# Two first w1 blocks between the scalings of v of steps 0 and 2, v of step 1 scaled on VectorE, v of block 1 in quarters, 40 leading zero matmuls

## The chip, the cores and the metric

One core of a Trainium2 chip runs the whole kernel. The metric is device time in microseconds: 230.68 us is the median of four runs before the change (231.03, 228.87, 230.79, 230.57). The profiled execution took 231.03 us, of which 228.8 us is the span from its first to its last recorded instruction.

## The reference

The inputs are q, k and v of 4 batches, 8 heads, 768 positions and 64 features, one decay `lam` per head, and two weight matrices. A linear attention with decay comes first, then a feed-forward layer:

```python
for b in range(nb):                      # blocks of 64 positions
    intra = einsum('bhic,bhjc->bhij', qb, kb) * Dmask          # lam ** (i - j), i >= j
    intra = einsum('bhij,bhjd->bhid', intra, vb)
    inter = einsum('bhid,bhde->bhie', qb * lam_pow, kv_state)
    out[:, :, sl] = intra + inter
    kv_state = lam_block * kv_state + einsum('bhsd,bhse->bhde', kb * rev_pow, vb)
x = out.transpose(0, 2, 1, 3).reshape(3072, 512)
h = x @ w_in                             # 512 x 2048
s = sin(alpha * h)
return (h + s * s / (alpha + 1e-9)) @ w_out                    # 2048 x 512
```

## The kernel before

**Tiling.** The kernel works on blocks of 128 positions and on pairs of batches. A block of a pair with one half of the heads is a "step"; there are 24, and steps 0 and 1 are the two head halves of block 0, steps 2 and 3 those of block 1. For a step, TensorE transposes q and k (T, line 444), multiplies them (S, line 453), and VectorE or ScalarE writes the transposes to `qkT` (line 623) and the masked product to `S_m` (line 568, or, for step 3 alone, ScalarE to `S_raw` at line 564 and VectorE at line 565). Then come the outputs of the step: `S_m` times the scaled v (line 466), the state from earlier blocks (line 476), and the new state from k and the scaled v (line 489). VectorE puts the output, with its decay, into `xT` (line 581) and adds up the state in `Zacc` (line 602); the next block reads the state as `Zs`.

**Scaling of v.** `prep_v(s)` (line 416) multiplies the v of step s, 128 x 512 float32 as it was loaded, by a table of decays `Lv` and writes it as bfloat16 to `v2`. It is one instruction (line 423) on the engine that the call names: POOL (GpSimd) or VectorE. Without it the output part of step s can't start.

**Feed-forward.** Four steps make a chunk of 512 tokens. `grp_A` multiplies `xT` of the chunk by 128 columns of w1 (four matmuls of 128x512, line 640), ScalarE takes the sine (line 644), one of three engines squares it (lines 651, 652) and VectorE forms `gT` (line 654); a chunk has 16 such groups. `grp_B` multiplies `gT` by w2 (line 677). Chunk 0 needs `xT` of steps 0 to 3, so its stage A ends the opening.

**Loads.** In the opening every large load is issued by POOL: k and q of blocks 0 and 1, v of blocks 0 and 1 (`load`, line 298), and w1 in four blocks (`w1_block`, line 405), which convert float32 to bfloat16 on the way. One issue occupies POOL's sequence about as long as a short computation. v of block 0 comes in quarters (`by_step=True`: two halves of the heads, each in two batches), v of block 1 in halves, by batch.

**Order.** No loop decides what an engine runs next. The program records operations with an estimated duration; `Program.add` gives each a planned start from its dependencies, the engine's free time and a model of the loads, and every engine's instructions are then sorted by planned start. Lines 715 to 760 record the opening by hand. An engine works through its list in order and waits on semaphores. `sec` records one or more parts of steps (t transposes, s product, o output); with `later=True` it hands back the part for VectorE and ScalarE as a function to call later. `P.ops[-1]` is the operation recorded last; a load given `after=[...]` waits for it.

`idle_pe(n)` (line 379) records n matmuls of 128x128 by 128 columns on a tile of zeros at the start; nothing reads their result.

Of the kernel before, what the change touches and what calls it, by code (L numbers as in the profile page):

```python
# [27 lines left out]
class Program:  # L28
# [57 lines left out]
    def add(self, eng, fn, dur, reads=(), writes=(), slot=None, nbytes=0, after=()):  # L86
        op = Op(eng, fn, dur, len(self.ops))
        self.ops.append(op)
        op.deps = self.deps_of(reads, writes) | set(after)
        for b in reads:  # L90
            if b.startswith("b."):
                op.deps.update(r for r in self.readers.get(b, ()) if r.eng != eng)
        for b in reads:
            self.readers.setdefault(b, []).append(op)
        for b in writes:
            self.writer[b] = op
            self.readers[b] = []
        op.nbytes = nbytes
        t = self.ready(eng, op.deps)
        if slot is None:  # L100
            op.start = self.place(eng, t, dur)
            op.end = op.start + dur
            return op
        op.slot = slot
        self.slots[slot] = self.slots.get(slot, 0) + 1
        op.kslot = self.slots[slot]
        issue = self.ISSUE[eng] * (0.85 if 10000 < nbytes < 100000 and eng == "POOL" else 1)
        op.start = self.place(eng, max(t, self.issued[eng]), issue)
        self.issued[eng] = op.start
        if nbytes < 10000:  # L110
            op.end = op.start + 2.9
        else:
            self.dma_free = max(self.dma_free, op.start + self.BEGIN) + nbytes / self.RATE
            op.end = self.dma_free + self.DONE
        return op
# [72 lines left out]
def bass_lightning_attn__then__act_snake_kernel(  # L188
# [31 lines left out]
    with es:  # L220
# [50 lines left out]
        P = Program()  # L271
        rec = P.add
        def bk(*ids):
            return [f"b.{i}" for i in ids]
# [9 lines left out]
        def fastest(choices, reads, writes, after=()):  # L284
            def end(c):
                eng, dur = c
                deps = P.deps_of(reads, writes) | set(after)
                return P.probe(eng, P.ready(eng, deps), dur) + dur
            return min(choices, key=end)

        def half(r):
            return slice(64 * r, 64 * r + 64)

        def where(s):
            pair, n, hh = s // 12, (s % 12) // 2, s % 2
            return pair, n, hh

        def load(d, x, after=(), by_step=False, eng=None, us=(0, 1)):
            pair, n = d // NB, d % NB
            r = d % RL  # L300
            src, dst = {"k": (k, k2), "q": (q, q2), "v": (v, v32)}[x]
            ops = []
            for h0, h1 in ((0, HS), (HS, H)) if by_step else ((0, H),):
                for u in us:
                    a = bass.AP(src.tensor, ((2 * pair + u) * H + h0) * S * D + n * BL * D,
                                [[2 * D, 64], [S * D, h1 - h0], [1, 2 * D]])
                    keys = [f"{x}.{r}.{u}.{h // HS}" for h in range(h0, h1, HS)]
                    op = rec(eng or ("SP" if x == "v" else "POOL"),
                             lambda e, u=u, a=a, h0=h0, h1=h1: e.dma_start(dst[r][half(u), h0:h1, :], a), 0,  # L309
                             writes=keys, slot=f"{x}{r}{h0 if by_step else ''}{'p' if eng else ''}",  # L310
                             nbytes=(187000 if d < 2 else 150000) if x != "v" else 216500 // (2 if by_step else 1), after=after)
                ops.append(op)
            return ops if by_step else op
# [6 lines left out]
        def consts():  # L320
            rec("ACT", lambda e: e.dma_start(lam_bc[:, :], bass.AP(lam.tensor, 0, [[0, 128], [1, H]])), 0,
                writes=["lam"], slot="lam", nbytes=4096)
            rec("ACT", lambda e: e.preload_act_table_set("natural_log_exp_and_others"), 1.3, writes=["table"])
            rec("ACT", lambda e: e.dma_start(alpha_r[:, :], moe_alpha.rearrange("(m p) -> m p", p=128)), 0,
                writes=["alpha_r"], slot="alpha", nbytes=8192)
            rec("DVE", lambda e: e.memset(maskf[:, :], 0.0), 0.2, writes=["maskf"])
            rec("ACT", lambda e: e.activation(lnlam[:, :], lam_bc[:, :], ACTF.Ln), 0.3,
                reads=["lam", "table"], writes=["lnlam"])
            for c in range(2):
                rec("ACT", lambda e, c=c: e.activation(lnlamp[half(c), :], lam_bc[half(c), c:H:2], ACTF.Ln), 0.3,  # L330
                    reads=["lam", "table"], writes=[f"lnlamp.{c}"])
# [13 lines left out]
        def iotas():  # L345
            rec("POOL", lambda e: e.iota(X_i[:, :, :], [[1, 2], [2, 64]], base=0, channel_multiplier=0), 0.2,
                writes=["X_i"])
            rec("POOL", lambda e: e.iota(N_i[:, :], [[BL, NB]], base=0, channel_multiplier=0), 0.1, writes=["N_i"])
            rec("POOL", lambda e: e.iota(E_i[:, :, :, :], [[BL, NB], [0, H], [1, 2]], base=0, channel_multiplier=2), 0.2,
                writes=["E_i"])  # L350

        def identf_op():
            rec("POOL", lambda e: e.affine_select(
                out=identf[:, :], in_=maskf[0:NM, 0:NM], pattern=[[-1, NM]], compare_op=ALU.not_equal, fill=1.0,
                base=0, channel_multiplier=1), 0.3, reads=["maskf"], writes=["identf"])
# [23 lines left out]
        def idle_pe(n):  # L379
            z = maskf[:, :].bitcast(BF16)  # L380

            def pe(e):
                for _ in range(n):
                    last = e.matmul(PS[:, 0, 0:128], z[:, 0:128], z[:, 128:256])
                return last
            rec("PE", pe, 0.06 * n, reads=["maskf"], writes=bk(0))
# [15 lines left out]
        def w_load(fn, keys, slot, n, after):  # L402
            return rec("POOL", fn, 0, writes=keys, slot=slot, nbytes=131072 * n, after=after)

        def w1_block(m0, n, after=()):
            cs = slice(128 * m0, 128 * (m0 + n))
            src = moe_w_in[:, cs].rearrange("(c p) f -> p c f", p=128)
            return w_load(lambda e: e.dma_start(w1[:, :, cs], src), [f"w1.{m}" for m in range(m0, m0 + n)],
                          f"w1_{m0}", n, after)
# [6 lines left out]
        def prep_v(s, engs=("POOL", "DVE")):  # L416
            pair, n, hh = where(s)
            c, r = s % RC, s // 2 % RL
            src = v32[r][:, HS * hh:HS * hh + HS, :].rearrange("p h (t d) -> p (h t) d", t=2)
            L_b = bass.AP(Lv, (n * H + HS * hh) * 2, [[NB * H * 2, 128], [1, 2 * HS], [0, D]])  # L420
            reads, writes = part_keys("v", s) + ["Lv"], [f"v2.{c}"]
            eng, dur = fastest([(e, {"POOL": 1.05, "DVE": 0.65}[e]) for e in engs], reads, writes)
            rec(eng, lambda e: e.tensor_tensor(v2[c][:, :, :], src, L_b, ALU.mult), dur, reads=reads, writes=writes)  # L423
# [7 lines left out]
        def part_keys(x, s):  # L431
            return [f"{x}.{s // 2 % RL}.{u}.{s % 2}" for u in range(2)]
# [282 lines left out]
        load(0, "k")  # L715
        load(0, "q")
        consts()
        idle_pe(16)
        iotas()
        consts3()  # L720
        load(1, "k")
# [3 lines left out]
        sec(t=1, tb=(2, 3), t_engs=("ACT",))  # L725
        consts2()
        load(0, "v", eng="POOL", by_step=True)
        load(1, "v", eng="POOL")
        identf_op()
        decay_table(0, 2)  # L730
        sec(s=0, sb_=4)
# [2 lines left out]
        sec(t=3, tb=(2, 3), t_engs=("ACT",))  # L734
        decay_table(2, NB)
        prep_v(0, ("POOL",))
        prep_v(1, ("POOL",))
        zl = []
        sec(s=2, sb_=0)
        o0 = sec(o=0, ob=4, z_late=zl, later=True)  # L740
        w1_block(0, 3, after=[P.ops[-1]])
        w1_block(3, 5)
        sec(s=3, sb_=2, via=True)
        o0()
        sec(o=1, ob=6, z_late=zl)
        prep_v(2, ("POOL",))
        prep_v(3, ("POOL",))
        w1_block(8, 4)
        w1_block(12, 4)
        o2 = sec(o=2, ob=0, later=True)  # L750
        o3 = sec(o=3, ob=2, later=True)
# [120 lines left out]
```

## Time and profile before

| quantity | us |
|---|---|
| median of four runs | 230.68 |
| profiled execution | 231.03 |
| its span | 228.8 |
| TensorE matmuls busy | 207.1 (91%) |
| VectorE busy | 144.0 (63%) |
| ScalarE busy | 125.1 (55%) |
| POOL busy, DMA issues among it | 117.7 (51%) |
| first matmul of stage A of chunk 0 starts | 23.44 |
| stage B of chunk 0 starts | 40.34 |

The page gives busy times over the whole span, then forty slices of it. TensorE is busy for nine tenths or more of nearly every slice from the fifth on; in the first four (some 5.7 us each) it is not. The timeline of an engine lists its instructions with start, duration, line and count; a bracket gives the idle time ahead of a group and what ended it. The chain of waits lists, in order of time, the work that each later piece had to wait for.

### The profile page before, as it was taken

The page shows a single profiled execution, that of the slowest core. Times are in us where ns is not written, and L with a number is a line of the kernel's source. Part 1 is how long each engine was busy: PE and PEld are TensorE (multiplying, and loading weights), DVE is VectorE, ACT ScalarE, POOL GpSimd, SP SyncE. Part 2 cuts the span into 40 slices and gives each one's busy share as a digit, 9 for nine tenths or more (in the row PEclk, how much of TensorE's full clock was granted, in tenths as well). Part 3 has the DMA queues.
Part 4 walks back from the last instruction along what each step waited for, and adds up shares of the span by engine and source line. Part 5 has one row for each costly group of instructions (what it writes and reads, how often), then busy time and mean ns, then how long its engine had stood idle before and what let it go on. Part 6 is the DMA issues. An engine that isn't in the chain of part 4 may idle for free.

```text
span 228.8 us, 6389 instructions
## 1 busy us (share of the span) xinstructions
PE 207.1 (91%) x2784; PEld 107.9 (47%) x2817; DVE 144.0 (63%) x205; ACT 125.1 (55%) x194; POOL 117.7 (51%) x154
## 2 busy tenths in 40 slices
PE   3465999989999989999999999999999999999994
PEld 2354343454544455644455544465544554444453
DVE  2764489548379957658765678766478764378400
ACT  4853389341399833477826477634577442568130
POOL 8978991233446554375664476653465500555300
PEclk9999999999999999999999999999999999999999
DMA  7959999972899985950179930198200104101033
GB/s 68 158 148 145 206 186 191 250 131 25 105 176 258 187 81 147 154 127 0 46 69 168 185 91 3 46 84 198 49 0 1 46 6 95 46 0 46 3 92 92
DMA packets 42891, 23.49 MB, mean 103 GB/s; under 512 B 26848, under 2 KB 39408, under 8 KB 42864
## 3 DMA queue, kind: packets, MB, share of 16 engines
q0 software_dynamic: 30240, 12.59, 43.6%
q1 hardware_dynamic: 12368, 10.42, 18.2%
q8 instruction: 22, 0.36, 0.7%
q10 hardware_dynamic: 256, 0.08, 0.2%
q14 instruction: 5, 0.04, 0.1%
HBM read 27.28 MB, written 6.29 MB: 147 GB/s over the span
## 4 chain that ended last, share of the span: by engine, by line
PE 78%; DVE 9%; POOL 5%; issue 3%; DMA 2%; ACT 1%; POOLq 0%; DVEq 0%
PE PS L677 32%; PE PS L640 31%; DVE gT L654 5%; PE PS L444 5%; PE PS L476 3%; PE PS L466 3%; PE PS L453 2%; DMA v<-in_v_dram 2%; DVE u L652 2%; PE PS L704 2%; POOL k L309 1%; PE PS L489 1%; POOL v L423 1%; DVE S_m L568 1%; POOL q L309 1%
## 5 line engine op out<-in xcount | busy, mean ns | idle before, releaser
L640 PE MATMUL PS<-xT,w 128*128 128x512 bf16 x376 | 88.5, 388 | 1.5 <-DVE Zacc L602 1.0
L654 DVE SCALAR_TENSOR_TENSOR gT<-u,r_sb,PS 128x512 bf16<-128x512 bf16 x96 | 69.7, 746 | 25.4 <-POOL u L652 21.7
L677 PE MATMUL PS<-w,gT 128*128 128x512 bf16 x343 | 81.9, 379 | 3.8 <-issue 3.6
L644 ACT ACTIVATE t<-PS,alpha_sb 128x512 bf16<-128x512 f32 x96 | 63.6, 682 | 22.8 <-PE PS L640 22.4
L652 POOL TENSOR_TENSOR u<-t 128x512 bf16<-128x512 bf16 x44 | 45.4, 1051 | 35.2 <-ACT t L644 32.3
L640 PEld LDWEIGHTS PS<-xT,w 128*128 128x128 bf16 x384 | 37.4, 100 | 49.3 <-issue 4.9
L677 PEld LDWEIGHTS PS<-w,gT 128*128 128x128 bf16 x368 | 33.9, 98 | 39.6
L568 DVE TENSOR_TENSOR S_m<-PS,mask 128x1024 bf16<-128x1024 f32 x23 | 28.1, 1224 | 22.1 <-PE PS L453 22.1
L623 ACT COPY qkT<-PS 128x1024 bf16<-128x1024 bf16 x21 | 21.2, 1011 | 28.8 <-PE PS L476 19.2
L684 ACT COPY osb<-PS 128x512 f32<-128x512 f32 x23 | 13.5, 585 | 29.5 <-PE PS L677 29.4
L309 POOL DMA_DIRECT2D k<-in_k_dram x24 | 16.9, 709 | 19.0 <-PE PS L677 12.5
L423 POOL TENSOR_TENSOR v<-v,Lv 128x512 bf16<-128x512 f32 x16 | 17.0, 1070 | 18.0 <-DMA v<-in_v_dram 16.9
L581 DVE TENSOR_TENSOR xT<-PS,Xt 128x512 bf16<-128x512 f32 x24 | 16.4, 685 | 11.7 <-PE PS L476 10.9
L444 PE MATMUL PS<-ident,q 64*64 64x64 bf16 x384 | 14.3, 205 | 6.7 <-POOL ident L316 5.0
L309 POOL DMA_DIRECT2D q<-in_q_dram x24 | 16.6, 701 | 5.7 <-PE PS L677 4.1
L651 ACT ACTIVATE u<-t 128x512 bf16<-128x512 bf16 x28 | 17.6, 630 | 1.4
L466 PE MATMUL PS<-S_m,v 64*64 64x128 bf16 x384 | 14.3, 235 | 3.6 <-POOL v L423 3.3
L652 DVE TENSOR_TENSOR u<-t 128x512 bf16<-128x512 bf16 x24 | 14.6, 610 | 4.4 <-ACT t L644 4.4
L444 PEld LDWEIGHTS PS<-ident,q 64*64 64x64 bf16 x384 | 9.6, 114 | 16.5 <-issue 11.9
L604 POOL CAST Zs<-Zacc 128x256 bf16<-128x256 f32 x16 | 7.5, 472 | 17.2 <-DVE Zacc L602 17.2
L476 PE MATMUL PS<-qkT,Zs 64*64 64x128 bf16 x160 | 15.5, 232 | 0.4
L453 PE MATMUL PS<-qkT 64*64 64x128 bf16 x384 | 12.6, 233 | 1.4 <-DVE qkT L623 0.8
(50 smaller groups left out, 129.5 us busy)
## 6 DMA issues: line engine op xcount, KB each, us to landing
out_dram<-osb SPq DMA_DIRECT2D x46, 128.0 KB, 2.8
v<-in_v_dram SPq DMA_DIRECT2D x16, 256.0 KB, 4.9
k<-in_k_dram POOLq DMA_DIRECT2D x24, 128.0 KB, 4.0
q<-in_q_dram POOLq DMA_DIRECT2D x24, 128.0 KB, 4.3
w<-in_moe_w_out_dram POOLq DMA_DIRECT2D x4, 512.0 KB, 12.5
v<-in_v_dram POOLq DMA_DIRECT2D x6, 256.0 KB, 12.3
w<-in_moe_w_in_dram POOLq DMA_DIRECT2D x2, 512.0 KB, 8.5
w<-in_moe_w_in_dram POOLq DMA_DIRECT2D x1, 640.0 KB, 7.4
```

The source lines that it names most:

```text
L309: lambda e, u=u, a=a, h0=h0, h1=h1: e.dma_start(dst[r][half(u), h0:h1, :], a), 0,
L423: rec(eng, lambda e: e.tensor_tensor(v2[c][:, :, :], src, L_b, ALU.mult), dur, reads=reads, writes=writes)
L444: last = e.transpose(dst, part((q2, k2)[x], t, u, h, tt), ident[half(u), half(u)])
L466: return e.matmul(dst, v2[o % RC][half(u), hid(h, tj), :], S_m[o % RS][half(u), h % 2 ^ u, h // 2, tj, :], start=start, stop=True, skip_gr ...
L476: return e.matmul(dst, Zs[(o - 2) % 3][half(r), u, h // 2, :], qkT[o % RQ][half(r), u, 0, h // 2, :], start=start, stop=True, skip_group_c ...
L568: rec("DVE", lambda e: e.tensor_tensor(s_out, s_in, mask_b, ALU.mult), 1.25, reads=keys_s + ["mask.0", "mask.1"], writes=[f"S_m.{s % RS}"])
L623: rec(eng, lambda e: (e.copy if eng == "ACT" else e.tensor_copy)(to, ti), dur, reads=keys_t, writes=[f"qkT.{j}"])
L640: last = e.matmul(PS[:, i, :], w1[:, kc, 128 * m:128 * (m + 1)], xT[x][:, kc, :], start=(kc == 0), stop=(kc == NKC - 1))
L644: rec("ACT", lambda e: e.activation(t16[tt][:, :], PS[:, i, :], ACTF.Sin, scale=alpha_sb[:, m:m + 1]), 0.7, reads=bk(i) + ["alpha"], write ...
L652: return e.tensor_tensor(u16[tt][:, :], t16[tt][:, :], t16[tt][:, :], ALU.mult)
L654: rec("DVE", lambda e: e.scalar_tensor_tensor(out=gT[g][:, m, :], in0=u16[tt][:, :], scalar=r_sb[:, m:m + 1], in1=PS[:, i, :], op0=ALU.mul ...
L677: last = e.matmul(PS[:, bank, :], gT[g][:, m, 128 * s4:128 * (s4 + 1)], w2[:, m, :], start=(m == 0), stop=(m == NM - 1))
```

## The change

Four edits in the opening and one in the model of issue times:

- `idle_pe(16)` becomes `idle_pe(40)`.
- v of block 1 is loaded in quarters, as v of block 0 is: four issues of 128 KB on POOL for two of 256 KB.
- The scaling of v for step 1 goes from POOL to VectorE; it is recorded after the product of step 2.
- w1 is loaded in blocks of 4, 4, 4 and 4 groups for 3, 5, 4 and 4. The first two are issued right after the scaling of step 0 (the first waits for it), the third waits for the scaling of step 3. Before, the first waited for the last TensorE operation of the output of step 0.
- In the model, an issue of 10,000 to 120,000 bytes on POOL counts 0.82 of the usual time; before it was 0.85, up to 100,000 bytes. Only the quarters of v, at 108,250 bytes, fall under the new bound.

`s3 = sec(..., later=True)` followed at once by `s3()` records the same operations in the same order as the one call did.

```diff
-        issue = self.ISSUE[eng] * (0.85 if 10000 < nbytes < 100000 and eng == "POOL" else 1)
+        issue = self.ISSUE[eng] * (0.82 if 10000 < nbytes < 120000 and eng == "POOL" else 1)
...
-        idle_pe(16)
+        idle_pe(40)
...
-        load(1, "v", eng="POOL")
+        load(1, "v", eng="POOL", by_step=True)
...
         prep_v(0, ("POOL",))
-        prep_v(1, ("POOL",))
+        w1_block(0, 4, after=[P.ops[-1]])
+        w1_block(4, 4)
         zl = []
         sec(s=2, sb_=0)
+        prep_v(1, ("DVE",))
         o0 = sec(o=0, ob=4, z_late=zl, later=True)
-        w1_block(0, 3, after=[P.ops[-1]])
-        w1_block(3, 5)
-        sec(s=3, sb_=2, via=True)
+        s3 = sec(s=3, sb_=2, via=True, later=True)
+        s3()
         o0()
         sec(o=1, ob=6, z_late=zl)
         prep_v(2, ("POOL",))
         prep_v(3, ("POOL",))
-        w1_block(8, 4)
+        w1_block(8, 4, after=[P.ops[-1]])
         w1_block(12, 4)
```

## The prediction, made before the changed kernel was run

> **What bounds the kernel now.** I read the forty slices of the page first:
>
> ```profile
> PE   3465999989999989999999999999999999999994
> ```
>
> From the fifth slice (22.9 us) TensorE is full almost throughout. Work that begins earlier there ends earlier; only the opening has room. So next comes the chain of waits of the opening:
>
> ```profile
> 8.72 1.77 POOL v L309 x3
> 10.49 4.79 DMA v<-in_v_dram
> 15.28 0.07 issue
> 15.35 1.04 POOL v L423
> 16.39 1.57 POOL w L408 x2
> 17.97 1.44 POOL v L423
> 19.41 0.04 issue
> ...
> 22.29 0.69 DVE xT L581
> 22.98 0.34 DVE Zacc L602
> 23.32 0.12 issue
> 23.44 6.16 PE PS L640 x15
> ```
>
> POOL carries the chain from 15.35 to 19.41 us: it scales v of step 1, issues two w1 loads, scales v of step 2. TensorE's output of step 2 waits for that. Then steps 2 and 3 run, and stage A of chunk 0 begins at 23.44. POOL's timeline shows its neighbours:
>
> ```profile
> 8.63 3.91 POOL L309 DMA_DIRECT2D v<-in_v_dram  x6
> 12.47 0.19 POOL L353 TENSOR_SCALAR_AFFINE_SELECT identf<-maskf 16x16 f32<-16x16 f32 x1
> 14.10 1.04 POOL L423 TENSOR_TENSOR v<-v,Lv 128x512 bf16<-128x512 f32 x1 [1.44 <-DMA v<-in_v_dram]
> 15.35 1.04 POOL L423 TENSOR_TENSOR v<-v,Lv 128x512 bf16<-128x512 f32 x1 [0.21 <-DMA v<-in_v_dram]
> 16.39 1.58 POOL L408 DMA_DIRECT2D w<-in_moe_w_in_dram  x2
> 17.96 2.45 POOL L423 TENSOR_TENSOR v<-v,Lv 128x512 bf16<-128x512 f32 x2
> ```
>
> The bracket 1.44 is idle time before step 0's scaling. The last line is steps 2 and 3: 1.44 us and 1.04 us by the chain and the row's median.
>
> A second loss lies inside stage A. TensorE's timeline there:
>
> ```profile
> 26.42 2.95 PE L640 MATMUL PS<-xT,w 128*128 128x512 bf16 x7
> 28.56 2.75 PE L640 MATMUL PS<-xT,w 128*128 128x512 bf16 x11
> ```
>
> Up to about 28.7 us a 128x512 matmul follows the last every 0.43 us, afterwards every 0.22 us, though the page's row of granted clock reads 9 throughout. From 23.44 to 28.7 only some 12 matmuls run, three groups of 16.
>
> [...] 5.3 us of stage A pass at half rate, then the rate doubles; the 16 zero matmuls (1.17 to 3.06 us) released nothing. [...] step 2's scaling took 1.44 instead of 1.04 us, and VectorE's `S_m` from `S_raw` (line 565, two SBUF inputs) lay over its first 0.54 us (17.96 to 18.50).
>
> **Part by part, against the profiled 231.03 us** (0.35 above the median of 230.68).
>
> *Quarters of v.* Two more issues at 0.68 us (the opening's median) make 1.35 us on POOL. They end at 12.66 + 1.35 = 14.0, still before 14.10, when step 0's v has landed: cost nothing, cover 1.44 us. If the cover were gone, POOL would be up to 1.35 late. SP's queue has nothing then. v of step 2 was issued third in order; its second quarter at about 12.0 with the opening's longest landing of 5.0 gives 17.0 at worst and some 16.3 by the order behind step 1's v (landed 15.28). Step 3's last issue, about 13.3, plus 4.1 (the median) gives 17.4.
>
> *Step 1 to VectorE.* POOL loses 0.21 of waiting and 1.04 of work, 1.25 us. VectorE pays 0.68 (its one scaling in the trace at line 423 took 681 ns). In its list the product of step 2 comes before (14.08 to 15.31) and `xT` of step 0 after (16.13): the scaling runs 15.35 to 16.03, in a gap of 0.82, and costs nothing. Without that gap it would delay `xT` by 0.68, which isn't read before 23 us. TensorE's output of step 1 waited until 16.45, but step 3's product, started 15.86, comes before it on TensorE and lasts to about 16.4: no gain there.
>
> *w1 between.* Four issues before, four after, 0.79 each; the first two now begin at about 15.14 for 16.39. The dependency on step 0's scaling replaces one on TensorE and is met as POOL gets there. So step 2's scaling starts at 17.96 - 1.25 = 16.71. It meets line 565 at 17.57, since step 3's chain through ScalarE doesn't move. By then 0.86 of 1.04 us is done; the remaining 0.18 go at the rate seen before (0.14 us of work in 0.54), so 0.69: end 18.26 for 19.41, **1.15 us earlier**. Step 3's scaling loses another 0.18 and ends at 19.48 for 20.41. TensorE's step 2 starts at 18.31 and step 3, 1.24 us behind as before (19.46 to 20.70), at 19.55. All that follows up to stage A keeps its lengths: stage A at 22.29. Bounds: 1.65 without any contention, 0.9 if step 3's scaling sets the pace.
>
> *First w1 block.* The 384 KB landed 4.8 us after issue (21.2) and the 640 KB, issued 0.8 later, 7.4 after (24.6): 3.4 us for 640 KB. 512 KB take 2.7 for 2.0 us, so it lands at 15.14 + 4.8 + 0.7 = 20.6, the second at 23.4: 1.7 us ahead of stage A. The later loads of w1, w2, k, q and v follow on POOL about 1.1 us earlier, as their users do. The wait of the third w1 block for step 3's scaling holds up nothing: POOL runs it in that order anyway. The changed issue model only orders; its effect on later choices of engines I put at zero, +-0.5.
>
> *Zero matmuls.* 24 more at 0.105 us (15 steps in 1.89 less the last one's 0.31) end at about 5.6, before the first transpose at 8.07: cost nothing. What they bring is unknown: below it is bounded by zero (clock stays half) and by a clock that is full from then until stage A. In that case steps 2 and 3 shorten: the pair's second part took 1.54 at half rate (20.70 to 22.24), and 1.02 in step 5, at 54.44 us, at full rate; step 3 can't start before its v at 19.48, so 0.5 counts. Stage A saves 5.27 - 12.3 x 0.216 = 2.6. VectorE's pace, 1.85 us for two groups, stays behind TensorE's 0.86 for one, but the eight banks absorb it. Sum 1.15 + 0.5 + 2.6 = 4.3 us; at most 1.65 + 0.5 + 3.1 = 5.3, where 3.1 is stage A now (23.44 to 40.34, 16.9) less 16 groups at 0.86. The loads have room: v of step 4 landed at 44.48 and is read at 52.25.
>
> I take zero as likeliest: 40 zero matmuls last 4.3 us, [...]2.5 us of idleness follow, then transposes with short products, any of which may lose the clock again before 22 us. What is late next is stage A at half rate.
>
> **The rivals.**
> - *A, the POOL gain alone*: 1.15 us (0.9 to 1.65), thus **229.5** from the median. 42%.
> - *B, the clock is released early and stays*: 4.3 us, 226.4 (down to 225.4). For it: [...]no gap between matmuls in the opening after 8 us exceeds 2.2 us. Against it: the sparse work there never released the clock. 39%[...].
> - *C, nothing arrives*: step 2's v or its `Zs` (ScalarE, 17.44 to 17.76) holds TensorE as long as POOL did; 230.7 +- 0.5. Only a landing at 18 or later would do it. 8%.
> - *D, slower*: stage A waits for w1. The quarters put more transfers ahead of it on one queue and its first block is a third bigger. w1 landings between 4.8 and 9.4 us occurred; at 9.4 the first block lands at 24.6, stage A starts 1.2 later than before: 231.9. It decides from a landing past 23.44, 8.3 us after issue; to exceed 1% it must pass 25.7, with second and later blocks late as well. Against it: the long landings had other w1 blocks ahead of them. 11%, 8% of it past 1%.
>
> **Numbers.** About 1% (2.3 us) is what measuring can tell from no change here. Faster by more: B, 0.39. Within: A, C and the rest of D, 0.53. Slower: 0.08. Predicted is A, 229.5. The range runs from B's bound, 225.4, to C's upper end, 231.2, and leaves out D and little else.
>
> **What would show it.** Right: POOL's list as scaling, two w1, two scalings from about 16.7, two w1; VectorE's scaling near 15.35; TensorE's step 2 at about 18.3; stage A at 22.3 with some 12 matmuls at 0.43. B shows as weight loads of 98 instead of 150 ns ahead of stage A and its start near 21.8. Wrong: a wait of stage A for w1, a DMA releaser ahead of the scaling of step 2 or 3, or POOL still idle before step 0's scaling for over 0.3 us.

## The result and the profile after

| | before | after |
|---|---|---|
| median, us | 230.39 (56 runs) | 229.01 (35 runs) |
| ratio of times | | 0.9948, 95% interval 0.9934 to 0.9963 |
| profiled execution, us | 231.03 | 229.91 |
| its span, us | 228.8 | 227.7 |
| stage A of chunk 0 starts | 23.44 | 22.38 |
| stage B of chunk 0 starts | 40.18 | 38.27 |

The change is 0.5% faster: 1.38 us between the medians, where 1.15 was forecast. The ratios here and below leave out runs more than 1.5% above the fastest of their kernel (one of the changed kernel, two of the six of `fill22`, five of the 20 of `v_halves`), the medians include them. Runs of one kernel differ by more than the change gains (227.98 to 231.87 us after it), so a single profile shows where time goes, and only medians and ratios show what is gained. (The timeline dates the first stage B matmul at 40.18 us in the kernel before; 40.34 in the opening table is the chain's figure.)

POOL's timeline in the changed kernel answers to the one shown of before (start, duration, line, count, idle time ahead):

```profile
8.63 5.00 POOL L309 DMA_DIRECT2D v<-in_v_dram  x8
13.54 0.19 POOL L353 TENSOR_SCALAR_AFFINE_SELECT identf<-maskf 16x16 f32<-16x16 f32 x1
14.06 1.04 POOL L423 TENSOR_TENSOR v<-v,Lv 128x512 bf16<-128x512 f32 x1 [0.33 <-DMA v<-in_v_dram]
15.40 1.57 POOL L408 DMA_DIRECT2D w<-in_moe_w_in_dram  x2 [0.30 <-POOL v L423]
16.96 2.53 POOL L423 TENSOR_TENSOR v<-v,Lv 128x512 bf16<-128x512 f32 x2
```

The two further v issues took most of the old idle time; the scaling of step 0 is where it was. The pair of scalings starts at 16.96 for 17.96. New is 0.30 us in which POOL waits for its own scaling before it issues w1. On VectorE the scaling of step 1 stands between the product of step 2 and `xT` of step 0, which began at 16.13 before:

```profile
14.14 1.23 DVE L568 TENSOR_TENSOR S_m<-PS,mask 128x1024 bf16<-128x1024 f32 x1 [0.75 <-PE PS L453]
15.29 0.68 DVE L423 TENSOR_TENSOR v<-v,Lv 128x512 bf16<-128x512 f32 x1
16.09 0.69 DVE L581 TENSOR_TENSOR xT<-PS,Xt 128x512 bf16<-128x512 f32 x1
```

TensorE's output of step 2, in the kernel before and then in the changed one:

```profile
19.46 0.64 PE L466 MATMUL PS<-S_m,v 64*64 64x128 bf16 x16 [2.16 <-POOL v L423]
18.09 0.64 PE L466 MATMUL PS<-S_m,v 64*64 64x128 bf16 x16 [1.01 <-ACT Zs L591]
```

The chain of waits now passes elsewhere:

```profile
16.01 0.46 PE PS L453 x11
16.50 1.01 ACT S_raw L564
17.51 0.56 ACT Zs L591 x2
18.09 0.64 PE PS L466 x16
...
21.23 0.69 DVE xT L581
21.92 0.34 DVE Zacc L602
22.26 0.12 issue
22.38 5.38 PE PS L640 x15
```

Step 2 starts at 18.09 for 19.46. Two waits now end almost together: POOL has scaled its v at 18.04, and ScalarE has written `Zs`, which stands behind `S_raw`, at 18.07. Two rows of the page, TensorE's busy share and its granted clock in forty slices, show the zeros:

```profile
PE   7366999999999799899999999999999999999994
PEclk9855699999999999999999999999999999999999
```

The second row was all nines before:

```profile
PEclk9999999999999999999999999999999999999999
```

In the windows view (stretch, length, TensorE busy and count, granted clock, DMA) the clock is full, then half, and full again inside stage A:

```profile
6.20:9.40 3.20, 0.75 (x64) 0.98 1.43 138
9.60:15.00 5.40, 2.80 (x112) 0.50 0.94 222
15.00:22.38 7.38, 5.11 (x162) 0.50 0.86 133
22.38:26.40 4.02, 4.02 (x10) 0.51 1.22 188
26.60:38.27 11.67, 11.46 (x53) 1.00 1.43 187
```

So after the 40 zeros, which end at 5.62 us, the granted clock was full from 5.9 to 9.3 us only. It was full again from 26.3 us, 4.0 after the start of stage A; in the profile of before this took some 5.5 (the clock is recorded as full from 29.0). Stage A is 15.9 us long for 16.7. Thus stage B started 1.91 us earlier, and 0.9 of that was lost in chunk 1: stage A of chunk 2 starts 0.98 us earlier (95.59 for 96.57), and about so it stays to the end.

The early full clock didn't come in every run. The time ahead of the first change that a trace records counts as full: the mean granted clock of the profile of before is 1.00, with the first change at 29.0 us. Six runs of the changed kernel have a mean of 1.00 too, as nearly all of the kernel before have, so no early change was recorded in them; in the others it is 0.955 to 0.963. The median of the six is 229.6 us, that of the others 228.9. This isn't a test of the zeros, since when the clock returns in stage A differs between runs as well.

### The profile page after: what moved, and what is told of

Read it like the earlier page. It is cut to its first block, busy times and chain, and to the rows that moved or that the text cites. A ratio compares the mean times of both kernels' runs of the same rounds, so it can differ in the third digit from the quotient of the medians.

```text
span 227.7 us, 6439 instructions
## 1 busy us (share of the span) xinstructions
PE 208.6 (92%) x2808; PEld 110.1 (48%) x2841; DVE 144.6 (63%) x206; ACT 125.0 (55%) x194; POOL 117.8 (52%) x155
## 3 DMA queue, kind: packets, MB, share of 16 engines
q1 hardware_dynamic: 12368, 10.42, 18.2%
## 4 chain that ended last, share of the span: by engine, by line
PE 78%; DVE 10%; POOL 4%; issue 3%; DMA 2%; ACT 2%; POOLq 0%
PE PS L677 32%; PE PS L640 30%; DVE gT L654 5%; PE PS L444 5%; PE PS L466 3%; PE PS L453 3%; PE PS L476 3%; DVE u L652 2%; DMA v<-in_v_dram 2%; PE PS L704 2%; POOL k L309 1%; PE PS L489 1%; POOL q L309 1%; DVE S_m L568 1%; ACT t L644 1%
## 5 line engine op out<-in xcount | busy, mean ns | idle before, releaser
L640 PE MATMUL PS<-xT,w 128*128 128x512 bf16 x376 | 87.6, 385 | 1.5 <-DVE Zacc L602 1.0
L423 POOL TENSOR_TENSOR v<-v,Lv 128x512 bf16<-128x512 f32 x15 | 16.1, 1080 | 18.3 <-DMA v<-in_v_dram 17.1
L466 PE MATMUL PS<-S_m,v 64*64 64x128 bf16 x384 | 14.2, 235 | 2.3 <-POOL v L423 1.1
## 6 DMA issues: line engine op xcount, KB each, us to landing
w<-in_moe_w_out_dram POOLq DMA_DIRECT2D x4, 512.0 KB, 13.6
v<-in_v_dram POOLq DMA_DIRECT2D x4, 256.0 KB, 14.2
```

The source lines that it names most:

```text
L466: return e.matmul(dst, v2[o % RC][half(u), hid(h, tj), :], S_m[o % RS][half(u), h % 2 ^ u, h // 2, tj, :], start=start, stop=True, skip_gr ...
L640: last = e.matmul(PS[:, i, :], w1[:, kc, 128 * m:128 * (m + 1)], xT[x][:, kc, :], start=(kc == 0), stop=(kc == NKC - 1))
```

## The experiments

Each kernel's ratio is to the kernel before, run on the same chip beside it.

**Zeros alone, and everything but the zeros.** `z16` is the changed kernel, `before_z40` the kernel before, each with one edit:

```diff
-        idle_pe(40)
+        idle_pe(16)
```

> The changed kernel with 16 zero matmuls instead of 40. Theory (the gain is POOL's shorter list, the clock has nothing lasting from the zeros): the median stays within 0.3 us of the changed kernel's 229.0, stage A of chunk 0 starts at 22.4 us as there, only the first transposes (8.2 us) run at half rate. Rival (the zeros are worth the 0.85 us by which stage A is shorter in the changed kernel's profile): about 229.9[...].

> The kernel before with 40 zero matmuls and nothing else. Theory (no lasting effect of the zeros): ratio to the kernel before 0.998 to 1.002, stage A at 23.4 us, the clock back at half before 12 us. Rival (the zeros carry a part of the gain): 0.6 to 0.9 us faster, a ratio of 0.996 to 0.997.

`z16`: 229.15 us, ratio 0.9965 (0.9945 to 0.9985). `before_z40`: 230.06 us, 1.0024 (0.9991 to 1.0058); its clock was full from 4.4 to 7.8 us and back at half until 28.3 (mean granted clock 0.955). The mean is 0.999 or 1.00 in all 22 runs of `z16`; in 11 of the 14 of `before_z40` it is 0.946 to 0.962, in three 0.993. So in most runs with 40 zeros the clock was full early, and in none with 16 was that recorded. Zeros by themselves gain nothing that shows. With 16 zeros the changed kernel is still faster than the kernel before; its interval overlaps that with 40, and the 0.4 us between the two ratios (0.9948 and 0.9965; up to 1.2 us by the ends of the intervals) stay unresolved. In the profile of `z16` stage A begins late for another reason, as TensorE's timeline shows:

```profile
23.16 2.29 PE L640 MATMUL PS<-xT,w 128*128 128x512 bf16 x5 [2.03 <-DMA w<-in_moe_w_in_dram]
```

That is my rival D's wait: its first w1 block landed some 8 us after issue. It came in an execution whose clock is recorded as full from 26.0 us, 2.9 after stage A's start. Stage B began at 38.80, half a microsecond later than in the changed kernel's profile, and yet this execution wasn't longer (229.10 for 229.91 us). How long after stage A's start the full clock comes differs between executions, from 2.9 us here to 6.0 in `v_halves` (without denser work ahead of it); no run shows that 16 or 40 zeros decide it.

**Step 1 back on POOL.** `step1_pool` is the changed kernel with

```diff
-        prep_v(1, ("DVE",))
+        prep_v(1, ("POOL",))
```

> The changed kernel with v of step 1 scaled on POOL again; it then comes after the first two w1 issues. Theory (POOL's list is the path): step 1's output about 1.6 us later than in the changed kernel, the scalings of steps 2 and 3 about 1.05 us later (18.0 and 19.1 us), stage A at 23.4 us, the median near 230.1. Rival (ScalarE's chain through S_raw and Zs is the path, POOL has slack): under 0.3 us slower than the changed kernel.

230.14 us, ratio 1.0016 (0.9984 to 1.0047): the gain is gone. Stage A starts at 23.46. The scalings of steps 1 to 3 run back to back on POOL, and TensorE waits for those of steps 1 and 2:

```profile
17.29 3.53 POOL L423 TENSOR_TENSOR v<-v,Lv 128x512 bf16<-128x512 f32 x3
```

```profile
18.42 0.64 PE L466 MATMUL PS<-S_m,v 64*64 64x128 bf16 x16 [1.65 <-POOL v L423]
19.88 0.64 PE L466 MATMUL PS<-S_m,v 64*64 64x128 bf16 x16 [0.60 <-POOL v L423]
```

**Step 1 on VectorE alone.** `before_dve` makes the same move in the kernel before and nothing else.

```diff
-        prep_v(1, ("POOL",))
+        prep_v(1, ("DVE",))
```

> The kernel before with v of step 1 scaled on VectorE and nothing else; the planner then puts this scaling ahead of the masked product of step 2, and xT of step 0 behind that of step 3. Theory (the place in VectorE's list decides, since Zs of step 0 follows xT of step 0): step 2 waits for Zs until about 19 us though its v is scaled by 18.5, stage A at 22.8 to 23.2 us, the ratio to the kernel before 0.998 to 1.001. Rival (taking one scaling from POOL is what counts): stage A at 22.4 us, a ratio of 0.995.

230.63 us, ratio 1.0021 (1.0000 to 1.0042): no gain, at most a small loss. POOL had v of step 2 scaled by 18.2, and yet step 2 started at 20.95. VectorE's timeline in the kernel before:

```profile
16.13 0.69 DVE L581 TENSOR_TENSOR xT<-PS,Xt 128x512 bf16<-128x512 f32 x1 [0.83 <-PE PS L489]
17.57 0.93 DVE L565 TENSOR_TENSOR S_m<-S_raw,mask 128x1024 bf16<-128x1024 bf16 x1 [0.75 <-ACT S_raw L564]
```

In `before_dve` VectorE's, then ScalarE's:

```profile
16.79 3.02 DVE L565 TENSOR_TENSOR S_m<-S_raw,mask 128x1024 bf16<-128x1024 bf16 x1 [0.64 <-ACT S_raw L564]
19.72 1.27 DVE L581 TENSOR_TENSOR xT<-PS,Xt 128x512 bf16<-128x512 f32 x2
```

```profile
20.44 0.37 ACT L591 CAST Zs<-PS 128x256 bf16<-128x256 f32 x1 [3.41 <-DVE xT L581]
```

`xT` of step 0 now stands behind the product of step 3, which took 3.02 us beside POOL's scalings (0.93 in the kernel before, also beside one), and `Zs` follows `xT`, since both read one bank, and the program lets its engines read a bank only one after the other. The theory held in kind, not in size: stage A began at 24.90, where 22.8 to 23.2 was expected, 1.5 us later than in the kernel before. The clock returned at 28.8 us, for 29.0 there, and stage B began only 0.65 us later (40.83).

**The two moves without quarters, zeros and new model.** `dve_w1` is the kernel before with

```diff
-        prep_v(1, ("POOL",))
+        w1_block(0, 3, after=[P.ops[-1]])
+        w1_block(3, 5)
         zl = []
         sec(s=2, sb_=0)
+        prep_v(1, ("DVE",))
         o0 = sec(o=0, ob=4, z_late=zl, later=True)
-        w1_block(0, 3, after=[P.ops[-1]])
-        w1_block(3, 5)
```

> The kernel before with v of step 1 scaled on VectorE, recorded after the product of step 2, and the two w1 loads (3 and 5 groups) right after the scaling of step 0; v of block 1 in halves, 16 zeros, the old model. VectorE's list comes out as in the changed kernel. Theory (these two moves are the whole gain): stage A at 22.0 to 22.5 us, the ratio to the kernel before 0.994 to 0.997, the same as the changed kernel's 0.995. Rival (quarters or zeros carry half of it or more): a ratio of 0.998 or more.

229.58 us, ratio 0.9972 (0.9953 to 0.9990), stage A at 21.91 us. By point estimates it has a little over half of the gain; the intervals (0.9953 to 0.9990, 0.9934 to 0.9963) overlap, so whether quarters and zeros hold the rest isn't decided by the times. For the opening the profiles say more, see below. In this profile the v of block 1 came in halves and no scaling waited for it.

**Halves in the changed kernel.** `v_halves`:

```diff
-        load(1, "v", eng="POOL", by_step=True)
+        load(1, "v", eng="POOL")
```

> The changed kernel with v of block 1 in two issues of 256 KB as before. Theory (the quarters only use POOL's idle time ahead of the scaling of step 0 and gain nothing): POOL idle 1.4 us ahead of that scaling again, all else within 0.1 us up to stage A, the time within 0.3 us. Rival (the quarters bring v of step 2 in time): a wait for v ahead of the scaling of step 2, stage A up to 0.5 us later.

230.54 us, ratio 0.9997 (0.9976 to 1.0018): the gain is gone, against both expectations. The profile is that of a long execution (233.00 us, in which the clock was at half once more from 83.3 to 86.7 us), so only the order and the waits of its opening are read here. A wait for v of 0.51 us came ahead of step 2's scaling, but that isn't what held step 2. TensorE's timeline and ScalarE's:

```profile
19.10 0.64 PE L466 MATMUL PS<-S_m,v 64*64 64x128 bf16 x16 [2.30 <-ACT Zs L591]
```

```profile
18.59 0.37 ACT L591 CAST Zs<-PS 128x256 bf16<-128x256 f32 x1 [1.33 <-DVE xT L581]
```

On VectorE the product of step 3 now stands ahead of `xT` of steps 0 and 1:

```profile
16.41 1.55 DVE L565 TENSOR_TENSOR S_m<-S_raw,mask 128x1024 bf16<-128x1024 bf16 x1 [0.51 <-ACT S_raw L564]
17.87 1.27 DVE L581 TENSOR_TENSOR xT<-PS,Xt 128x512 bf16<-128x512 f32 x2
```

Two issues of 256 KB for four of 128 KB give POOL other planned times, and the planner put `xT` of step 0 behind the product of step 3 again, as in `before_dve`. In `dve_w1`, with halves too, it didn't, and the gain was there. So the quarters matter in the changed kernel by the order that they lead to. The new factor of 0.82 isn't needed for it: with the old one all five engines' lists come out the same. No run moves `xT` alone.

How much each opening gains shows when it is counted from the start of POOL's first scaling, because v of step 0, for which that waits, came at different times in these executions (12.93 us in `v_halves`, 14.39 in `step1_pool`). From there to stage A it is 9.34 us in the kernel before, 8.32 in the changed one and 8.31 in `dve_w1`: in these profiles the two moves alone give the whole gain up to stage A. In `step1_pool` it is 9.07. In `v_halves` it is 9.79 and in `before_dve` 11.59: where `xT` stands a place later, the opening is longer than before the change.

**The two waits left at step 2.** `no_after_zs` is the changed kernel with

```diff
-        w1_block(0, 4, after=[P.ops[-1]])
+        w1_block(0, 4)
...
-        w1_block(8, 4, after=[P.ops[-1]])
+        w1_block(8, 4)
...
-                if part != 1 and (no > 0 or o == 0):
+                if part != 1 and no > 0:
                     put_x()
...
-                if no == 0 and o > 0:
+                if no == 0:
                     put_x()
```

> The changed kernel without the two explicit dependencies of w1 loads on the scalings before them, and with Zs of step 0 written before xT of step 0. Theory (the changed kernel's step 2 waits for two things at once, POOL's list, in which the dependency costs 0.30 us twice, and Zs behind S_raw on ScalarE): w1 issued at 15.1, step 2 at 17.8 for 18.1, stage A at 22.0 to 22.1, 0.3 us faster than the changed kernel. Rival (another wait sets step 3, its S_m or the product of step 2): stage A unchanged at 22.4.

228.59 us, ratio 0.9960 (0.9932 to 0.9988); by the ratio not to be told from the changed kernel. Its profile has step 2 at 17.78 and stage A at 21.60, but v landed 0.4 us earlier in it too; counted as above the opening takes 7.93 us for 8.32. The 0.30 is gone:

```profile
13.67 1.04 POOL L423 TENSOR_TENSOR v<-v,Lv 128x512 bf16<-128x512 f32 x1
14.66 1.57 POOL L408 DMA_DIRECT2D w<-in_moe_w_in_dram  x2
```

**Zeros in TensorE's idle stretches.** `fill` adds to the changed kernel 9 matmuls of zeros at each of two places (`fill` is `idle_pe` with a bank to write):

```diff
         sec(o=1, ob=6, z_late=zl)
+        fill(9, 0)
...
         alpha_ops(4)
+        fill(9, 6)
```

> The changed kernel with 9 zero matmuls more after the output of step 1 and 9 more ahead of stage A, in TensorE's two idle stretches of 1.0 us. Theory (the clock is kept at half by idleness, and dense work of any form before stage A releases it): the full clock comes at about 20 us, stage A starts at 21.9 and takes 13.9 instead of 15.9 us, so 2 to 2.5 us faster than the changed kernel, 226.5 to 227. Rival[...]: clock released as before, after about 4 us of stage A; within 0.3 us of the changed kernel.

In the opening it went as the clock theory says: full clock from 17.7 us (mean granted clock 0.978), stage A at 21.09, stage B at 35.34, 4.8 us earlier than in the kernel before. But the time was 230.52 us, ratio 1.0027 (1.0004 to 1.0049). By stage A of chunk 2 only 1.0 of the 4.8 us was left. In stage B of chunk 0 TensorE's timeline has gaps that no engine explains:

```profile
44.95 0.41 PE L462 MATMUL PS<-qkT 64*64 64x128 bf16 x13 [0.77 <-issue]
50.65 0.59 PE L686 MATMUL PS<-w,gT 128*128 128x512 bf16 x2 [0.69 <-issue]
```

and one of 1.26 us at 92.9. The three make 2.7 of the 3.8 us lost; a wait for VectorE's `gT` at the end of stage A of chunk 1 (1.40 us, 0.65 in the kernel before) makes most of the rest. Counted in TensorE's recorded instructions in this trace the three stand at 1204, 1459 and 2729: 255 apart, and 5 x 254. A trace also records a DMA queue of kind "instruction" (on the changed kernel's page `q8 instruction: 22, 0.36`, packets and MB, so some 16 KB each); in that of `fill` a piece of 16,384 bytes began on it at 42.38, 48.34 and 91.09 us, 1.6 to 1.8 us ahead of each gap. (Most of the 22 stand ahead of no gap.) From these places and times alone I guessed that the gaps are late fetches of TensorE's own instructions; no view shows whose instructions a piece holds. I put the list back to its length with fewer leading zeros (`fill22`, the kernel `fill` with the first edit below), or lengthened it without filling (`z58`, the changed kernel with the second):

```diff
-        idle_pe(40)
+        idle_pe(22)
```

```diff
-        idle_pe(40)
+        idle_pe(58)
```

> As the kernel with 18 zero matmuls in the two idle stretches, but with 22 leading zeros for 40: TensorE's list is as long again as in the changed kernel[...]. Theory (the 4.9 us gained by the start of stage B were given back to fetches that fell into bursts of small instructions; their place decides): stage B of chunk 0 starts at 35.2 to 35.6 us, no gap named issue over 0.5 us on TensorE before 60 us, 226.5 to 227.5 us. Rival (the gaps come because stage B now runs while the loads of w2, k, q and v still fill the DMA queues): the same gaps of 0.7 us and more as with 40, the median over 229.5.

> The changed kernel with 58 leading zero matmuls: TensorE's list is as long as in the kernel with 18 zeros in the idle stretches, but stage A isn't earlier. Theory (place of the fetches): stage A at 22.4 us as in the changed kernel, then gaps named issue of 0.5 us and more in stage B of chunks 0 and 1, and 1 to 2 us slower than the changed kernel. Rival (the gaps come from stage B being early against the loads): no such gaps, within 0.3 us of the changed kernel.

`fill22`: 228.18 us in six runs, ratio 0.9877 (0.9821 to 0.9934). In its profile, of one of the faster of the six (226.94 us), the clock is full from 19.7 us, the two gaps in stage B of chunk 0 and that at 92.9 are gone, and of 4.4 us gained by the start of stage B 4.0 last to the end:

```profile
15.00:19.90 4.90, 4.84 (x159) 1.00 0.79 107
20.00:21.50 1.50, 1.24 (x29) 1.00 1.24 205
21.60:35.50 13.90, 13.74 (x63) 1.00 1.34 194
```

(The first line's 1.00 isn't a measured clock, see the end.) `z58`: 229.62 us, 0.9972 (0.9952 to 0.9993), and no such gaps, against the expectation: its list is as long as that of `fill`, but stage B comes 2.7 us later. My estimate from these three profiles, one of each kernel, is that a gap took both, an unlucky place in the list and an early stage B. That a fetch is its cause isn't shown, nor was it tried whether one queues behind the data loads. With the 58 zeros the clock was full from 5.7 to 12.5 us, and it too was back at half until 26.2 (mean granted clock 0.970).

**The parts together.** `best` joins the edits of `no_after_zs` with 6 zeros ahead of the output of step 1, 5 ahead of stage A, and 29 leading ones.

> The changed kernel with the two dependencies of w1 loads dropped, Zs of step 0 written before xT of step 0, 6 zero matmuls ahead of the output of step 1, 5 ahead of stage A and 29 leading ones, 40 in all. Theory (the clock, POOL's list and ScalarE's chain are three separate losses, and the length of TensorE's list keeps the fetches where they did no harm): stage A at 21.4 to 21.6 us with the full clock released before 23 us, stage B at 35.3 to 35.6 us, 226.3 to 227.3 us, a ratio to the kernel before of 0.984 to 0.988. Rival (gaps named issue or waits for w1 return as stage A comes earlier): over 228 us, with the loss visible as such gaps.

228.02 us in six runs, ratio 0.9892 (0.9849 to 0.9934), short of the expectation by 0.7 us: in its profile with the 11 zeros the clock wasn't full before stage A (half until 24.8 us). The rival's gaps didn't return: the longest named issue is 0.4 us, and stage A doesn't wait for w1. It and `fill22` are the fastest here, 1.1 to 1.2% below the kernel before; six runs can't rank them.

## Why the prediction was right, and where it wasn't

- **Bound and direction: right.** Case A said 229.5 us; 229.01 came. `step1_pool` shows that POOL's list is the path there: with step 1's scaling on POOL, behind the two w1 issues, the gain is gone. `before_dve` shows that a shorter list on POOL isn't enough.
- **Stage A's start: 22.29 forecast, 22.38 measured**, by errors that cancel. The dependency on step 0's scaling, "met as POOL gets there", cost 0.30 us, so the scaling of step 2 began at 16.96 for 16.71. I let the slow pace that the trace of before shows beside line 565 fall on step 2's scaling (1.55 us); it took 1.08 and step 3's took 1.53. So step 2 started at 18.09 for 18.31, and a wait for `Zs`, which I had kept for rival C, ended last ahead of it, by 0.03 us. Step 3's scaling ended at 19.49 for 19.48, and step 3 started at 19.64 for 19.55. That the total came within 0.1 us is luck in part.
- **Step 1 on VectorE: right**, at 15.29 for 0.68 us, in the gap named.
- **Quarters at nothing: right for POOL's time** (the two issues took 1.09 us for 1.35, and 0.33 of the idle 1.44 is left, at the edge of my own sign of being wrong, over 0.3), **wrong as an edit.** I put "its effect on later choices" at zero, +-0.5, and thought of choices of engines. `v_halves` and `before_dve` show that planned times move `xT` of step 0 by a place in VectorE's list. In both the gain is absent and step 2 waits for the `Zs` behind it.
- **Zeros at nothing: right in the median as far as the intervals go**, and the clock fell back to half where I put it, at 9.3 us: TensorE was busy for 0.75 of the 3.4 us in which it was full, and its longest stretch without a matmul ahead of that was 2.59 us. That 40 zeros might be enough, and that sparse work might lose the clock again, was my estimate: the trace of before shows neither. Half of rival B came true: the clock was full early. `fill22` shows what B's other half is worth: stage A 14.2 us long (21.55 to 35.79) and 1.2%, 2.8 us, in all, where I had put 4.3.
- **Rival D: its wait exists** (2.03 us in `z16`), but it didn't decide a median.
- **What I didn't forecast: 0.9 us given back in chunk 1.** In the changed profile three of VectorE's squares there took 1.17, 1.05 and 1.25 us beside POOL's scalings (1.18, 1.05 and 0.66 in the kernel before); TensorE waits 0.5 us longer for `gT` at the end of stage A, and 0.4 went at 94 us with a gap named issue. The first loss appears in some profiles here and not in others; why wasn't tried.

## What to carry to other kernels

Cost a moved instruction by what stands behind it in every list that it joins, and where a planner writes the lists, compare them after each edit, the edits of a load's size included: the move of step 1's scaling gained 0.3 to 0.5% in two kernels and nothing in two in which `xT` came a place later on VectorE. An early full clock, from 4.4 to 7.8 us in `before_z40`, gained nothing that shows (ratio 1.0024); with denser work up to stage A and a full clock from 19.7 us there was a gain (`fill22`, 0.9877), with one from 17.7 us none (`fill`, 1.0027). A gain in an opening should be followed through the next stages before it is believed: `fill` had 4.8 us at the first landmark and nothing at the end.

## What the runs showed of the hardware that I had not expected

- The page of the kernel before has a row of granted clock of all nines, while matmuls of 128x512 follow each other every 0.43 us up to some 29 us; the first change that its trace records is to full, at 29.0 us.
- In the changed kernel's trace the granted clock was full for 3.41 us (5.86 to 9.28) and then at half for 17.07 (9.28 to 26.34), five times as long. Worked out from the mean granted clocks and the spans of the profiled runs, the stretch at half was some 20.5 us in `before_z40` (0.955 of 228.1 us) and some 13.6 in `z58` (0.970 of 227.4 us), six and four times 3.41. Why, isn't shown.
- A DMA issue that depends on the computation before it on POOL itself cost 0.30 us of idle time, twice in the changed kernel; without the dependency (`no_after_zs`) none.
- VectorE's product of `S_raw` and the mask (line 565) took 0.93 us in the kernel before, 1.06 in the changed one, 1.70 in `best` and 3.02 in `before_dve`, each time beside POOL's scalings. Where it took 1.06, one scaling took 1.53; where it took 3.02, they kept to 1.04 to 1.08. What sets which of them slows, isn't shown.
- Three gaps on TensorE of 0.7 to 1.3 us in `fill` stood 255 of its recorded instructions apart, or a multiple of 254, 1.6 to 1.8 us after 16 KB pieces began on the trace's queue of kind "instruction". One profile shows them, and no run their cause.
